# Block maxima to the query stacks' rows by eight on-chip transfers, with no store to DRAM between

## The chip, the cores and the metric

One NeuronCore of a Trainium2 chip runs the kernel. The metric is the device time of one execution in microseconds (us), as the median of several runs. Engines are named as in the profile: PE (matrix multiply; PEld are its weight loads), DVE (vector), ACT (scalar, activation functions), POOL (GpSimd) and SP (the sync engine, which here does nothing but issue transfers).

## The reference

The input x is 2048 x 512 in float32. It is normalized over each row and goes to two branches, whose results are added to x:

```python
xn = _layernorm(x)
qkv = xn @ wqkv                      # 32 heads of 16 columns each for q, k and v
scores = einsum("bhqd,bhkd->bhqk", q, k) * 16 ** -0.5
o = einsum("bhqk,bhkd->bhqd", softmax(scores), v)
return x + (o @ wo) + (gelu(xn @ w1 + b1) @ w2 + b2)
```

w1 is 512 x 1792 and w2 is 1792 x 512. The softmax needs the maximum of each query's scores over all 2048 keys; this kernel subtracts it inside the score product, and the change is about the way of these maxima into that product.

## The kernel before

**Blocks and units.** The attention is cut into 32 blocks: 8 groups of 4 heads (`NG`) times 4 blocks of 512 queries (`NQB`, `QB`). Block t has 16 units, so there are `NU` = 512. `unit()` is called once per unit u and issues, in this order on the engines' queues, pieces of several stages. For unit u it makes the first scores, queries on the partitions (`s_half`: products `pS`), and DVE reduces them to maxima (`s_max`: `mt`, line 390). For unit e = u - 19 (`LEAD`) it makes the scores again, now keys on the partitions (`e_half`: products `pT`), which ACT turns into exponentials (`pe`, line 431). One or two units behind, `v_half` multiplies these with v (`pV`). Between them stand matmuls of the dense work (`dense`: `pD`): projections, then the MLP, then the output projection. All `tiled` products carry line 171 in the profile. The queues are first in, first out, so this order is what runs.

**The stacks.** q and k lie as float16 parts in `qst` and `kst`, tiles of 128 partitions: head parts in partitions 0 to 61 and 64 to 125, and two rows more in each half, 62 and 63 (a = 0), 126 and 127 (a = 1). In `kst` these two rows hold a constant. In `qst` they hold the negated block maximum of each query as a float16 and its remainder (j = 0, 1), so that the second score product subtracts the maximum by itself. `qst` is a set of four tiles per group, two sets in turn.

**The way of the maxima.** When the last unit of block t has been reduced, `s_end` has DVE reduce `mt` to `mx` (line 358); POOL scales it and splits it into two float16 parts (lines 360 to 362). `store()`, called in the unit after it, has PE turn them by two small products (`m_turn`, line 366), ACT copy the result to `mturned`, a tile of 64 partitions x 64 elements (`m_copy`, line 371), and SP issue three transfers: `m_store` (line 347) writes `mturned` to `m_d` in DRAM, and `m_rows` (line 352), once for a = 0 and then for a = 1, reads it back into rows 62 and 63, or 126 and 127, of the block's `qst` tile. A read waits for the store's landing. The first `e_half` of block t, two units and a half after the turn, needs these rows: its product n = 1 reads the half with rows 126 and 127, the next product, n = 0, the half with rows 62 and 63.

**The opening.** Everything up to unit 18 (normalization, first projections, scores of block 0, v) is put in order by `Plan`, a planner with a cost in ns for each step, a wire time for transfers (`size`, `LAG`) and a `tail` (what still has to follow, the longest first). For block 0 it holds `m_store` as a step of 420 ns and the two `m_rows` as steps of 270 ns behind it. From unit 19 on, `unit()` alone sets the order.

**Transfers.** All transfers of this program are issued by SP, in one order. Each takes the next of eight semaphores in turn, so the ninth issued waits until the first has landed. While the first unit of a block is under way the large transfers are held back (`held`).

Of the kernel before, what the change touches and what calls it, by code (L numbers as in the profile page):

```python
# [10 lines left out]
F16 = mybir.dt.float16  # L11
# [7 lines left out]
P = 128  # L19
# [9 lines left out]
NQB = S // QB  # L29
NG = H // 4  # L30
# [9 lines left out]
LAG, E_TAIL = 3000, 8000  # L40
# [15 lines left out]
def layer_kernel(ctx: ExitStack, tc: tile.TileContext, x, wqkv, wo, w1, b1, w2, b2, out):  # L56
    nc = tc.nc
# [3 lines left out]
    def pool(stack, name, bufs=1, space=None, side=None):  # L61
        kw = {k: v for k, v in (("space", space), ("side", side)) if v is not None}
        return stack.enter_context(tc.tile_pool(name=name, bufs=bufs, **kw))
# [4 lines left out]
    dram = pool(ctx, "dram", space=DRAM)  # L68
# [4 lines left out]
    w1_d = dram.tile([NF // 2, P, 2, 2, NC, P], F16, name="w1_d")  # L73
    w2_d = dram.tile([P, 2, NF, D], F16, name="w2_d")
    acc_d = dram.tile([S, D], F32, name="acc_d")
    m_d = dram.tile([NG * NQB, 2, 2, 2, 8, P // 2], F16, name="m_d")
    ot_d = dram.tile([D, 2, S], F16, name="ot_d")
    den_d = dram.tile([NG * NQB, 2, 4, QB], F32, name="den_d")

# [5 lines left out]
    kst, qst = ([[const.tile([P, 2, QB], F16, name=f"{x}st{i}_{b}") for b in range(NQB)] for i in range(2)] for x in "kq")  # L85
# [23 lines left out]
    def banks(tag):  # L109
        k = free_banks[tag].pop(0)  # L110
        free_banks[tag].append(k)
        return bank_tile(k, tag)
# [48 lines left out]
    def given(engine, ns):  # L161
        backlog[engine] += ns
# [54 lines left out]
    class Plan:  # L217
# [7 lines left out]
        def add(self, engine, ns, fn, after=(), take=(), free=(), size=0, tail=0, gap=0):  # L225
            t = dict(gap=gap, e=engine, ns=ns, fn=fn, after=[a for a in after if a], take=take, free=free, size=size, tail=tail,
                     end=None, n=len(self.todo))
            for key in free:
                self.users.setdefault(key, []).append(t)
            self.todo.append(t)  # L230
            return t
# [111 lines left out]
            slot[0] += 1  # L343
        slot[0] = now

    def m_store(t, turned):
        nc.sync.dma_start(m_d[t].rearrange("s a j r q -> (s a j r) q"), turned)

    def m_rows(t, a):
        g, qb = divmod(t, NQB)  # L350
        dst = qst[g % 2][qb][64 * a + 62:64 * a + 64].rearrange("j p (t s q) -> j (p t) s q", s=2, q=P // 2)
        nc.sync.dma_start(dst, m_d[t, :, a].rearrange("s j r q -> j r s q"))  # L352

    def m_parts(t):

        mx = work.tile([P, 2, 8], F32, name="mx", bufs=1)
        parts = work.tile([P, 2, 2, 8], F16, name="mparts", bufs=2)
        return (lambda: nc.vector.tensor_reduce(mx.rearrange("p a r -> p (a r)"), mt_of[t].rearrange("p h t k -> p (h t) k"),  # L358
                                                axis=AX.X, op=ALU.max),
                lambda: nc.gpsimd.tensor_scalar(mx, mx, 1.0 / MROW, 0.0, op0=ALU.mult, op1=ALU.add),  # L360
                lambda: nc.gpsimd.tensor_scalar(parts[:, :, 0], mx, 1.0, 0.0, op0=ALU.mult, op1=ALU.add),
                lambda: nc.gpsimd.tensor_tensor(parts[:, :, 1], mx, parts[:, :, 0], op=ALU.subtract)), parts

    def m_turn(pt, parts):
        for s in range(2):
            nc.tensor.matmul(pt[32 * s:32 * s + 32, :64], parts[64 * s:64 * s + 64].rearrange("p a j r -> p (a j r)"),
                             nident[64 * s:64 * s + 64], start=True, stop=True)

    def m_copy(pt):
        turned = work.tile([64, 64], F16, name="mturned", bufs=2)  # L370
        nc.scalar.activation(turned, pt[:64, :64], AF.Copy)
        return turned
# [26 lines left out]
    def s_end(u):  # L399

        t, i = divmod(u, 16)
        if i < 15:
            return
        steps, parts = m_parts(t)
        for step in steps:
            step()
        given("dve", 220)

        def store():

            fresh = cur[0] is not None and 0 < sum(cur[0].at) <= 4
            pt = banks("S" if fresh else "T")
            m_turn(pt, parts)
            m_store(t, m_copy(pt))
            for a in range(2):
                m_rows(t, a)

        stores[t] = store

# [417 lines left out]
    with ExitStack() as st1:  # L837
# [45 lines left out]
        add = plan.add  # L883
# [206 lines left out]
        for w in (1, 0):  # L1090
# [5 lines left out]
            else:  # L1096
                a = add("POOL", 800, lambda wf=wf, i1=i1: nc.gpsimd.tensor_scalar(tl[wf], tl[wf], i1, 0.0, op0=ALU.mult, op1=ALU.add), [h])
                w_ready[w] = add("POOL", 1100, lambda wf=wf, hi=hi, lo=lo: nc.gpsimd.tensor_tensor(lo, tl[wf], hi, op=ALU.subtract), [a], free=[wf])
        a = add("DVE", 90, lambda: nc.vector.tensor_tensor(sexp[:, 0:1], fac0[:, 0:1], fac0[:, 1:2], op=ALU.mult), [chain])
        a = add("DVE", 90, lambda: nc.vector.tensor_scalar_mul(sexp[:, 0:1], sexp[:, 0:1], DH ** -0.5), [a])  # L1100
# [5 lines left out]
        a = add("DVE", 90, lambda: nc.vector.tensor_tensor(amv[:, 2:3], amv[:, 0:1], amv[:, 1:2], op=ALU.max), v_sum)  # L1106
# [40 lines left out]
        mkey, m_of = ("S", "m", 0), []  # L1147
        m_steps, m0 = m_parts(0)
        a = add("DVE", 220, m_steps[0], m_last)
        for step in m_steps[1:]:  # L1150
            a = add("POOL", 220, step, [a])
# [4 lines left out]

        a = add("PE", 300, turn_m, [a], take=[mkey])
        a = add("ACT", 220, lambda: m_of.append(m_copy(tl[mkey])), [a], free=[mkey])
        put = add("SP", 420, lambda: m_store(0, m_of[0]), [a], size=4)
        for k in range(2):  # L1160
            add("SP", 270, lambda k=k: m_rows(0, k), [put], size=4, tail=E_TAIL)

        for t in range(NV):
            v_tile(t)
# [17 lines left out]
        for n, src in enumerate(every[:NM]):  # L1182
            key = ("wch", "m", n)
            dst = am_all[:, 12 + n:13 + n] if n < 2 else am_all[:, n - 2:n - 1] if n < 9 else amx[:, n - 2:n - 1]
# [342 lines left out]
```

## Time and profile before

| | before |
|---|---|
| median of 3 runs | 1458.85 us (1458.36 to 1459.63) |
| the profiled execution | 1460.86 us, of which the span is 1459.0 us |
| PE busy | 1433.1 us, 98% of the span |
| DVE busy | 1350.7 us, 93% |
| ACT busy | 1258.2 us, 86% |
| POOL busy | 683.3 us, 47% |
| transfers issued by SP in this path | 32 stores, 64 reads |
| granted TensorE clock | 0.997 |

A row of the groups reads: line, engine, operation, written tile <- read tiles, count; the durations are in ns. In the timeline a row is a start in us, a duration, and what ran; a bracket at its end holds the idle time of the engine just before it and what ended it. In the waits a row is who waited for whom, the sum in us, the times, and the longest. SP rows are issue times: how long the issuing took, not when the data landed.

### The profile page before, as it was taken

The numbers are of one execution on the slowest core, as the hardware profiler recorded it, in microseconds if no ns is written. First come the engines' busy times: TensorE is split into PE (matmuls) and PEld (weight loads), VectorE is DVE, ScalarE is ACT, GpSimd is POOL, SyncE is SP. The second block draws the span as 40 slices with busy tenths as digits, with TensorE's granted clock in tenths as the row PEclk, the third lists the DMA queues.
The fourth block names the chain that finished last, engine by engine and source line by source line (L and its number), as shares of the span: only waits on it lengthen the run. The fifth ranks groups of instructions, "written<-read, shape, count | busy, mean of one in ns | idle before, by whom it ended". The sixth has DMA issues, their size and how long they took to land.

```text
span 1459.0 us, 88559 instructions
## 1 busy us (share of the span) xinstructions
PE 1433.1 (98%) x40120; PEld 946.8 (65%) x40120; DVE 1350.7 (93%) x2240; ACT 1258.2 (86%) x2399; POOL 683.3 (47%) x769
## 2 busy tenths in 40 slices
PE   7999999999999999999999999999999999999998
PEld 4336666666666666666667666666666666666665
DVE  7979999999999999999999999999999999999933
ACT  5868888888999888899988889998889999888885
POOL 3201856754589511278752127784115778212110
PEclk9999999999999999999999999999999999999999
DMA  6740564545323111121112111131102210121423
GB/s 207 219 136 28 174 203 150 165 157 162 86 88 116 51 53 38 43 86 43 46 45 79 32 45 44 41 88 45 45 25 82 56 44 20 52 63 46 126 80 116
DMA packets 113010, 124.84 MB, mean 86 GB/s; under 512 B 23292, under 2 KB 84604, under 8 KB 112632
## 3 DMA queue, kind: packets, MB, share of 16 engines
q1 hardware_dynamic: 112632, 119.18, 26.8%
q8 instruction: 313, 5.13, 1.5%
q14 instruction: 65, 0.53, 0.1%
HBM read 81.66 MB, written 37.34 MB: 82 GB/s over the span
## 4 chain that ended last, share of the span: by engine, by line
PE 85%; DMA 6%; DVE 5%; ACT 3%; issue 1%; SPq 1%; DVEq 0%; ACTq 0%
PE pD L171 26%; PE pV L171 24%; PE pT L171 18%; PE pS L171 15%; DVE mt L390 3%; DMA m_d<-mturned 3%; DMA qst<-m_d 2%; ACT pe L431 1%; PE pT L1032 1%; SPq L352 1%; DMA qk_d<-stg 0%; DMA wq<-in_A_wqkv_dram 0%; DVE bs L970 0%; DMA kst<-qk_d 0%; DMA xs<-in_A_x_dram 0%
## 5 line engine op out<-in xcount | busy, mean ns | idle before, releaser
L390 DVE TENSOR_REDUCE mt<-pS 128x1 f32<-128x512 f32 x2029 | 1279.9, 684 | 46.4 <-PE pS L171 21.3
L431 ACT ACTIVATE pe<-pT 128x512 f32<-128x512 f32 x2048 | 1106.1, 599 | 154.2 <-PE pS L171 67.8
L171 PE MATMUL pV<-pe,vv 64*32 64x512 f32 x8192 | 1084.7, 591 | 0.1
L171 PE MATMUL pT<-qst,kst 64*32 64x512 f16 x8192 | 705.2, 378 | 9.2 <-DMA qst<-m_d 8.1
L171 PE MATMUL pS<-kst,qst 62*32 62x512 f16 x8116 | 619.2, 378 | 2.0 <-DVE mt L390 1.5
L171 PEld LDWEIGHTS <-qst 62*32 62x32 f16 x8192 | 303.5, 90 | 198.4 <-issue 47.9
L171 PE MATMUL pD<-xb,wc 64*32 64x512 f16 x5376 | 362.8, 375 | 0.0
L171 PE MATMUL pD<-w_s,g 64*32 64x512 f16 x5376 | 360.5, 375 | 0.0
L171 PEld LDWEIGHTS <-kst 64*32 64x32 f16 x8192 | 277.9, 91 | 115.1 <-issue 25.8
L171 PEld LDWEIGHTS pV<-pe,vv 64*32 64x32 f32 x8192 | 239.1, 105 | 14.2 <-PE pV L171 4.6
L171 PEld LDWEIGHTS <-wc 64*32 64x32 f16 x5376 | 158.2, 91 | 45.3
L171 PEld LDWEIGHTS <-g 64*32 64x32 f16 x5376 | 160.8, 91 | 39.9
L171 PE MATMUL pD<-xt,wqk_h 64*32 64x512 f16 x2400 | 159.9, 376 | 0.0
L360 POOL TENSOR_SCALAR mx<-mx 128x16 f32<-128x16 f32 x32 | 6.5, 204 | 303.9 <-DVE mx L358 293.1
L1369 POOL TENSOR_TENSOR xa<-xa,yt 128x512 f32<-128x512 f32 x16 | 20.5, 1284 | 156.2 <-ACT yt L1367 156.2
L171 PEld LDWEIGHTS <-wqk_h 64*32 64x32 f16 x2400 | 72.4, 92 | 20.9 <-issue 2.2
L1321 POOL TENSOR_TENSOR t<-hh 128x512 f32<-128x512 f32 x56 | 58.2, 1039 | 42.6 <-ACT hh L1344 40.5
L1323 POOL TENSOR_TENSOR t<-t,hh 128x512 f32<-128x512 f32 x56 | 71.7, 1281 | 4.7
L1316 POOL TENSOR_TENSOR t<-t,hh 128x512 f32<-128x512 f32 x56 | 71.7, 1280 | 4.6
L1318 POOL TENSOR_TENSOR g<-t,g 128x512 f16<-128x512 f32 x56 | 65.2, 1164 | 4.7
L488 POOL TENSOR_TENSOR osb<-osb,rb 128x512 f32<-128x512 f32 x31 | 39.9, 1286 | 38.8 <-DMA rb<-den_d 38.3
L171 PE MATMUL pD<-wo_s,oc 64*32 64x512 f16 x816 | 54.6, 376 | 0.0
(160 smaller groups left out, 934.7 us busy)
## 6 DMA issues: line engine op xcount, KB each, us to landing
wc<-w_d SPq DMA_DIRECT2D x56, 256.0 KB
qk_d<-stg SPq DMA_DIRECT2D x32, 256.0 KB
rb<-den_d SPq DMA_DIRECT2D x124, 64.0 KB
wch<-in_B_w_dram SPq DMA_DIRECT2D x14, 512.0 KB
wch<-in_B_w_dram SPq DMA_DIRECT2D x28, 256.0 KB
w_d<-wsp SPq DMA_DIRECT2D x28, 256.0 KB
kst<-qk_d SPq DMA_DIRECT2D x64, 96.0 KB
qst<-qk_d SPq DMA_DIRECT2D x64, 96.0 KB
```

The costliest lines, as they stand in the source:

```text
L171: p = nc.tensor.matmul(*args, **kw)
L352: nc.sync.dma_start(dst, m_d[t, :, a].rearrange("s j r q -> j r s q"))
L360: lambda: nc.gpsimd.tensor_scalar(mx, mx, 1.0 / MROW, 0.0, op0=ALU.mult, op1=ALU.add),
L390: nc.vector.reduce_max(mt_of[t][:, n // 2 + n % 2 * 2, qt, kb:kb + 1], s, axis=AX.X)
L431: nc.scalar.activation(pe, st, AF.Exp, scale=scale_of[g // 2])
L488: pooled((1280, lambda: nc.gpsimd.tensor_tensor(osb, osb, rb, op=ALU.mult)), (620, lambda: nc.gpsimd.tensor_scalar(ot[:, 0], osb, 1.0, 0.0 ...
L1032: nc.tensor.matmul(tl[key], lhs, rhs, start=c + n == 0, stop=(c, n) == (NC - 1, 2))
L1316: (1280, lambda: nc.gpsimd.tensor_tensor(t1, t1, hh, op=ALU.mult)),
L1318: (1160, lambda: nc.gpsimd.tensor_tensor(g[:, 1, f, :], t1, g[:, 0, f, :], op=ALU.subtract)),
L1321: pooled((1040, lambda: nc.gpsimd.tensor_tensor(t1, hh, hh, op=ALU.mult)), (620, lambda: nc.gpsimd.tensor_scalar(t1, t1, 1.0, 1.0 / GELU_A ...
L1323: (1280, lambda: nc.gpsimd.tensor_tensor(t1, t1, hh, op=ALU.mult)),
L1369: add = lambda: nc.gpsimd.tensor_tensor(xa, xa, yt, op=ALU.add)
```

## The change

The store to DRAM and its tensor `m_d` go. `m_rows` now moves straight from `mturned` to the `qst` rows, with a transfer for each half of the queries (s) and each row (j): 8 partitions x 64 elements of `mturned` become one row of 8 pieces of 64 elements. That is four transfers for each a, eight for a block in place of three, all from the SP queue, and a = 1 goes ahead of a = 0. The product n = 1 of the first `e_half` now waits for four transfers, as does n = 0, where each waited for one; and `m_copy`, when it writes `mturned` again two blocks later, waits for the eight that read it. In the planner the steps of 420 and twice 270 ns become two of 1100 ns, with nothing between `m_copy` and them.

```diff
-    m_d = dram.tile([NG * NQB, 2, 2, 2, 8, P // 2], F16, name="m_d")
...
-    def m_store(t, turned):
-        nc.sync.dma_start(m_d[t].rearrange("s a j r q -> (s a j r) q"), turned)
-
-    def m_rows(t, a):
+    def m_rows(t, turned, a):
         g, qb = divmod(t, NQB)
-        dst = qst[g % 2][qb][64 * a + 62:64 * a + 64].rearrange("j p (t s q) -> j (p t) s q", s=2, q=P // 2)
-        nc.sync.dma_start(dst, m_d[t, :, a].rearrange("s j r q -> j r s q"))
+        for s in range(2):
+            for j in range(2):
+                row, k = 64 * a + 62 + j, 32 * s + 16 * a + 8 * j
+                dst = qst[g % 2][qb][row:row + 1].rearrange("o p (t s q) -> o s (p t) q", s=2, q=P // 2)
+                nc.sync.dma_start(dst[:, s], turned[k:k + 8])
...
             m_turn(pt, parts)
-            m_store(t, m_copy(pt))
-            for a in range(2):
-                m_rows(t, a)
+            turned = m_copy(pt)
+            for a in (1, 0):
+                m_rows(t, turned, a)
...
         a = add("ACT", 220, lambda: m_of.append(m_copy(tl[mkey])), [a], free=[mkey])
-        put = add("SP", 420, lambda: m_store(0, m_of[0]), [a], size=4)
-        for k in range(2):
-            add("SP", 270, lambda k=k: m_rows(0, k), [put], size=4, tail=E_TAIL)
+        for k in (1, 0):
+            add("SP", 1100, lambda k=k: m_rows(0, m_of[0], k), [a], size=4, tail=E_TAIL)
```

After the opening the rows of PE, DVE, ACT and POOL stand as before; only SP's differ. First SP's queue at the end of the opening and at block 1, before (each number behind a tile's name is its buffer):

```order
L913 DMA wch<-in_A_wo_dram 128x2x512 x2
L347 DMA m_d<-mturned 64x64
L1059 DMA qk_d<-stg 128x512
L352 DMA qst_0_87<-m_d 2x16x64 x2
L1058 DMA qk_d<-stg 128x2x512
L536 DMA qst_2_89<-qk_d 48x2x512 x2
L536 DMA kst_0_83<-qk_d 48x2x512 x2
L1205 DMA xn_d<-xt 256x1x512
L347 DMA m_d<-mturned 64x64
L352 DMA qst_1_88<-m_d 2x16x64 x2
L536 DMA kst_1_84<-qk_d 48x2x512 x2
```

The same stretch of SP's queue with the change:

```order
L912 DMA wch<-in_A_wo_dram 128x2x512 x2
L1058 DMA qk_d<-stg 128x512
L351 DMA qst_0_86<-mturned 1x8x64 x8
L1057 DMA qk_d<-stg 128x2x512
L535 DMA qst_2_88<-qk_d 48x2x512 x2
L535 DMA kst_0_82<-qk_d 48x2x512 x2
L1203 DMA xn_d<-xt 256x1x512
L351 DMA qst_1_87<-mturned 1x8x64 x8
L535 DMA kst_1_83<-qk_d 48x2x512 x2
```

At block 1, as at every later block, a store and two reads have become eight row transfers in the same place; at block 0 they also stand behind a store of projections (`qk_d<-stg`) that the store of the maxima stood ahead of.

The opening is also planned anew: its rows on PE, DVE and ACT are the same work in another order up to the first `e_half`. ACT's queue around the copy of block 0's maxima (line 371), before:

```order
L921 ACTIVATE wch,amx<-wch 128x1024
L371 ACTIVATE mturned<-pS 64x64
L921 ACTIVATE wch,amx<-wch 128x1024
L1044 ACTIVATE stg<-pT 128x512
L1054 ACTIVATE pf<-pT 128x512
L1129 ACTIVATE vv<-pD 128x32x16
L921 ACTIVATE wch,amx<-wch 128x1024
L1129 ACTIVATE vv<-pT 128x32x16 x2
L431 ACTIVATE pe<-pT 128x512 x14
```

And with the change, where the copy is line 370:

```order
L920 ACTIVATE wch,amx<-wch 128x1024 x4
L1043 ACTIVATE stg<-pT 128x512
L1053 ACTIVATE pf<-pT 128x512
L1128 ACTIVATE vv<-pD 128x32x16
L370 ACTIVATE mturned<-pS 64x64
L920 ACTIVATE wch,amx<-wch 128x1024 x2
L1128 ACTIVATE vv<-pT 128x32x16 x2
L430 ACTIVATE pe<-pT 128x512 x14
```

The copy has moved behind the three results of projections (`stg`, `pf`, `vv`) that it stood ahead of, and so nearer to the first exponential (`pe`), which needs the rows.

## The prediction

> **What bounds the kernel now.** I read the page's shares and its chain first, then the waits, then the timeline at two block boundaries, one late and one on time.
>
> ```profile
> span 1459.0 us, 88559 instructions
> PE 1433.1 (98%) x40120; PEld 946.8 (65%) x40120; DVE 1350.7 (93%) x2240; ACT 1258.2 (86%) x2399; POOL 683.3 (47%) x769
> PE pD L171 26%; PE pV L171 24%; PE pT L171 18%; PE pS L171 15%; DVE mt L390 3%; DMA m_d<-mturned 3%; DMA qst<-m_d 2%; ACT pe L431 1%; PE pT L1032 1%; SPq L352 1%; DMA qk_d<-stg 0%; DMA wq<-in_A_wqkv_dram 0%; DVE bs L970 0%; DMA kst<-qk_d 0%; DMA xs<-in_A_x_dram 0%
> ```
>
> PE carries the time, with DVE close behind. The chain also passes through both transfers of the maxima, 5% of the span. That share is no gain by itself: while they fly, PE has other work. What PE really loses stands in the waits.
>
> ```profile
> DVE mt L390 <- PE pS L171: 23.2, 31, 2.5
> ...
> PEld L171 <- DMA qst<-m_d: 17.0, 18, 1.5
> ...
> PE pT L171 <- DMA qst<-m_d: 8.1, 12, 1.0
> ...
> SPq L347 <- ACT mturned L371: 290.6, 32, 39.3
> SPq L352 <- DMA m_d<-mturned: 54.7, 31, 2.9
> ```
>
> PE stood still for 8.1 us in all because the rows in `qst` were not there, at 12 of the 32 blocks, and its weight loads for 17.0 us at 18. SP itself waits 54.7 us for the landings of its own stores. Here is a late boundary, first SP, then PE's weight loads and matmuls:
>
> ```profile
> 977.88 0.47 SPq L347 DMA_DIRECT2D m_d<-mturned  x1
> 981.22 1.39 SPq L352 DMA_DIRECT2D qst<-m_d  x2
> ...
> 984.06 0.10 PEld L171 LDWEIGHTS <-kst 64*32 64x32 f16 x4 [1.45 <-DMA qst<-m_d]
> ...
> 984.06 0.40 PE L171 MATMUL pT<-qst,kst 64*32 64x512 f16 x4 [0.95 <-DMA qst<-m_d]
> ```
>
> And one on time:
>
> ```profile
> 760.72 2.60 SPq L679 DMA_DIRECT2D xb<-xn_d  x3
> 770.52 0.50 SPq L347 DMA_DIRECT2D m_d<-mturned  x1
> 772.25 1.37 SPq L352 DMA_DIRECT2D qst<-m_d  x2
> ...
> 775.34 0.42 PE L171 MATMUL pT<-qst,kst 64*32 64x512 f16 x4
> ...
> 775.64 0.41 PE L171 MATMUL pT<-qst,kst 64*32 64x512 f16 x4
> ```
>
> Counted from the start of the store, PE comes to the product n = 1 after 4.82 us (775.34 - 770.52) and to n = 0 after 5.12. At the late boundary n = 1 starts at 6.18, so 1.36 late, of which PE idles 0.95: the first 0.41 are covered by matmuls still running. The difference between the two is the store: its landing lets the reads go after 3.34 us there and 1.73 here. The stretches from one reduction of maxima to the next, with these two kinds of boundary:
>
> ```profile
> 726.10:768.30 42.20, 41.27 (x1233) 28.80 (x1222) 40.30 (x66) 37.02 (x71) 22.18 (x25) 1.00 0.14 39
> 768.30:809.00 40.70, 40.70 (x1230) 28.95 (x1222) 40.24 (x67) 35.61 (x68) 7.46 (x9) 1.00 0.27 79
> ```
>
> The first has a late boundary (PE busy 41.27 of 42.20), the second none (PE 40.70 of 40.70, DVE 40.24). So a late boundary costs its PE idle time or a little more, and a block without one is at the limit of PE and nearly of DVE: nothing below that is to be had.
>
> **The change, part by part.** *The removed store and its wait.* Every PE wait on `qst<-m_d` goes: 8.1 us by the PE row. DVE's waits for `pS` (23.2) bound the gain from above, since they hold other causes too; I take 8.1.
>
> *The eight transfers.* This is the term that decides. They start when the store started, run one behind the other on SP, and land some time after their issue ends. The landing: from the end of the store's issue (770.52 + 0.50) to the reads' start is 1.23 us; from the end of the second read's issue (981.22 + 1.39) to PE's start 1.45, with 32 pieces of 64 elements each. A row transfer has 8 pieces, so I take 1.2. With a pitch p from one issue to the next, the rows for n = 1 are there at 4p + 1.2, those for n = 0 at 8p + 1.2. No row of before has this transfer; its nearest:
>
> ```profile
> L469 SPq DMA_DIRECT2D den_d<-osb x124: 215/244/537, 148.9 to 1407.7; - x124
> ...
> L347 SPq DMA_DIRECT2D m_d<-mturned x32: 466/476/527, 87.3 to 1396.9; - x32
> ...
> L495 SPq DMA_DIRECT2D ot_d<-ot x124: 570/594/2279, 197.6 to 1430.6; - x124
> ...
> L352 SPq DMA_DIRECT2D qst<-m_d x64: 603/658/793, 89.9 to 1399.8; - x64
> ```
>
> The medians are 0.24 us for one whole row, 0.48 for plain partitions of 64 elements, 0.59 and 0.66 where source and destination are cut differently. Two reads take 1.39, so each costs 0.04 more than its own time. Then p is 0.28, 0.52, 0.63 or 0.70, and the rows for n = 0 come at 3.4, 5.3, 6.2 or 6.8 us, against a need of 5.12. For n = 1 the worst is 4.0 against 4.82: it never waits, which is the use of taking a = 1 first. n = 0 is late by 0, 0.2, 1.1 or 1.7; less 0.41 of cover PE idles 0, 0, 0.7 or 1.3 us a block, over 31 blocks (block 0 is in the opening) 0, 0, 22 or 39 us. The new transfer is cut differently on its two sides (8 partitions become one row) but has only 8 pieces, so I put it between the store and the `ot_d` row, nearer to the store: p = 0.53. Then n = 0 comes at 5.44, 0.32 late. That lies within the cover, so PE idles for nothing by this count; but running dry still costs some overlap, between 0 and 0.32 a block, 0 to 10 us. I take 4.
>
> *What stands behind.* SP's next transfers at the on-time boundary started 3.15 us after the store (772.25 + 1.37 + 0.04 - 770.52 at the earliest), and now start at 8p = 4.2; at the late boundary they started at 4.8. No PE wait on one of them is among the large rows, so 0. The semaphores: the eight take all eight, so the last can wait for a transfer issued before the first. At the on-time boundary the last large ones were issued by 763.32 (760.72 + 2.60), 7 us earlier, and the late store took 3.3 us to land: 0.
>
> *More waits on ACT and PE.* The copy on ACT now waits for up to eight landings of two blocks ago, PE for four in place of one:
>
> ```profile
> L371 ACTq EVENT_SEMAPHORE  x28: 17/17/17, 179.8 to 1396.1; - x28
> ```
>
> At 17 ns each, up to four more in front of the copy delay it by under 0.1 us a block, which lies within the bounds of p. On PE the same price for four more at a block's start is 0.07 us, 2 us in all at most; nothing below zero, as they only add. I take 0, because the weight loads ahead of them have idle time to give on most boundaries.
>
> *The opening.* It is the same work in another order.
>
> ```profile
> 87.02 0.22 ACT L371 ACTIVATE mturned<-pS 64x64 f16<-64x64 f32 x1 [0.95 <-PE pS L366]
> ...
> 89.83 0.61 ACT L1129 ACTIVATE vv<-pD 128x512 f32<-128x512 f32 x1
> ...
> 87.26 0.53 SPq L347 DMA_DIRECT2D m_d<-mturned  x1
> ...
> 90.00:100.00 10.00, 8.84 (x122) 3.43 (x125) 7.69 (x13) 3.94 (x8) 1.16 (x1) 1.00 0.34 107
> ...
> 96.60 0.39 PE L171 MATMUL pT<-qst,kst 64*32 64x512 f16 x4
> 98.15 0.41 PE L171 MATMUL pS<-kst,qst 62*32 62x512 f16 x8 [1.16 <-DVE mt L390]
> 98.37 0.40 PE L171 MATMUL pT<-qst,kst 64*32 64x512 f16 x4
> ```
>
> Before, n = 1 of block 0 came 9.3 us after the store's start and n = 0 11.1. The copy now stands behind three more ACT results, of which this `vv` is the last. It ended at 90.44, so measured on the old opening the copy comes 3.4 us later than 87.02. That leaves n = 1 at 5.9 us against 4p + 1.2 = 3.3, and n = 0 at 7.7 against 5.44: no wait. PE idles 1.16 us in the last 10 us of the opening, so a better order can give about that and a worse one take as much: 0, with 1.5 to either side.
>
> *The sum.* -8.1 + 4 + 0 = -4 us. The profiled execution took 1460.86 (span 1459.0 and 1.9 around it), so it would take 1457; the median of the runs, 1458.85, is 2.0 lower, and with the same 4 off gives 1455.
>
> **The rivals.** *The issue of eight becomes the wait (slower).* SP issues one after the other, and n = 0 waits at every block, also where before it was on time. It decides from a pitch of about 0.59: there PE idles 8 x 0.59 + 1.2 - 5.12 - 0.41 = 0.39 us a block, 12 in all, 4 more than the 8.1 won. At the `ot_d` row's pitch it is +14, 1473; at that of `qst<-m_d` +31, 1490. For it speaks that this row, with the same destination, is the dearest; against it that its transfers have four times the pieces. The Trainium skill (DMA: Bandwidth & Descriptors, "Rules for kernel authors") says of many small transfers that one should coalesce them, since below 64 KB one pays mostly overhead; by that rule three transfers in place of eight are right and this change goes the wrong way, to the 1473 to 1490 just worked out. The trace agrees so far that the issue price hardly follows the bytes (0.48 us for 8 KB, 0.66 for 4 KB). Against the rule stands that the three are two landings in a row and the eight only one.
>
> *A wash.* With p between 0.56 and 0.59, or with the uncovered loss at its full 0.3 us a block, what n = 1 wins n = 0 gives back: 1456 to 1462. The large row of DVE's waits speaks for less loss, as `pS` now stands ahead of the late product in PE's queue and DVE is fed.
>
> *The whole gain.* With p at or under 0.5, near the store's row or below, no boundary waits: 1458.85 - 8.1 = 1451, and 1449 with a good opening.
>
> **How the numbers follow.** A change under 0.2% (2.9 us) can't be told from none. The forecast, with the whole gain as its better end (1448 to 1456), has 0.45; the wash 0.20; the slow issue 0.35. So faster 0.45, same 0.20, slower 0.35. The forecast's own range is 1448 to 1456. The full range goes from 1448 to 1478, the slow issue up to a pitch of 0.65; that leaves out its upper third (0.12) and a little below.
>
> **What would show it.** In the profile after, the row of `qst<-mturned` gives the issue time (forecast 0.49 us) and its timeline the pitch. No boundary should wait at n = 1, which is the first `pT` of a block; a wait there means a landing far over 1.2 us or a held semaphore. A wait that is there should name `qst<-mturned` ahead of the second `pT`, be alike at all blocks, and make DVE wait less than before. The opening is right if the first `pT` still starts at 95 to 98 us. The forecast is wrong if the pitch is over 0.59, or if stretches like 726 to 768 do not come down towards 40.7 although PE no longer waits.

## The result, and the profile after

The changed kernel takes 1507.15 us, median of 4 runs (1505.59 to 1512.22), against 1458.61 (1458.12 to 1459.63) for the kernel before: a ratio of 1.0338, 95% interval 1.0311 to 1.0365. It is 48.5 us slower, where the prediction said 4 faster, and it lies outside the range (1448 to 1478). The page of the changed kernel, with the rows that answer to those shown of before:

```profile
span 1503.9 us, 88901 instructions
PE 1444.2 (96%) x40120; PEld 951.2 (63%) x40120; DVE 1353.3 (90%) x2240; ACT 1262.6 (84%) x2399; POOL 683.3 (45%) x769
PE pD L170 23%; PE pV L170 22%; PE pT L170 16%; PE pS L170 13%; SPq L351 9%; DMA qst<-mturned 4%; ACT pe L430 2%; DVE mt L389 1%; PE pT L1031 1%; PE pD L1031 0%; DMA wq<-in_A_wqkv_dram 0%; DVE bs L969 0%; DVE sd L971 0%; ACT mturned L370 0%; DMA xs<-in_A_x_dram 0%
```

DVE and ACT do the same work as before, in a longer span. New in the chain is SP's queue on line 351, the issue of the eight, with 9% of the span, and 4% for their landing. Before, the store and reads had 1% of issue (`SPq L352`) and 5% of landing. The waits say who pays:

```profile
PE pT L170 <- DMA qst<-mturned: 40.2, 31, 2.3
...
DVE mt L389 <- PE pS L170: 36.5, 35, 5.4
DVE mt L389 <- PE pT L170: 33.2, 40, 2.7
```

PE waits for the rows 31 times, at every block end but the opening's, 40.2 us in all (before 8.1 us, 12 times). DVE's waits for PE rise too, from 23.2 us for `pS` and 5.4 for `pT`. The row of the transfers, and one block end on SP and PE:

```profile
L351 SPq DMA_DIRECT2D qst<-mturned x256: 624/628/1552, 94.2 to 1445.7; - x128
```

```profile
790.79 5.47 SPq L351 DMA_DIRECT2D qst<-mturned  x8
796.31 0.57 SPq L678 DMA_DIRECT2D xb<-xn_d  x1
...
795.61 0.41 PE L170 MATMUL pT<-qst,kst 64*32 64x512 f16 x4
795.68 0.59 PE L170 MATMUL pS<-kst,qst 62*32 62x512 f16 x8
797.33 0.40 PE L170 MATMUL pT<-qst,kst 64*32 64x512 f16 x4 [1.07 <-DMA qst<-mturned]
```

Eight issues take 5.47 us, 0.68 each. The first `pT`, n = 1, starts 4.82 us after the first issue (795.61 - 790.79) and waits for nothing. The second, n = 0, starts after 6.54 us, which is 1.07 us after the end of the eighth issue. This is the block that was on time before the change. From one reduction of maxima to the next it took 40.70 us then, and takes 42.00 now, with PE busy for 40.93 of them:

```profile
788.60:830.60 42.00, 40.93 (x1230) 28.53 (x1219) 40.34 (x66) 35.56 (x68) 7.46 (x9) 1.00 0.27 77
```

### The profile page after: what moved, and what is told of

The parts are those of the page before. It is cut to its first block, busy times and chain, and to the rows that moved or that the text cites. A ratio compares the mean times of both kernels' runs of the same rounds, so it can differ in the third digit from the quotient of the medians.

```text
span 1503.9 us, 88901 instructions
## 1 busy us (share of the span) xinstructions
PE 1444.2 (96%) x40120; PEld 951.2 (63%) x40120; DVE 1353.3 (90%) x2240; ACT 1262.6 (84%) x2399; POOL 683.3 (45%) x769
## 4 chain that ended last, share of the span: by engine, by line
PE 77%; SPq 9%; DMA 4%; ACT 4%; DVE 3%; issue 2%; ACTq 0%; DVEq 0%
PE pD L170 23%; PE pV L170 22%; PE pT L170 16%; PE pS L170 13%; SPq L351 9%; DMA qst<-mturned 4%; ACT pe L430 2%; DVE mt L389 1%; PE pT L1031 1%; PE pD L1031 0%; DMA wq<-in_A_wqkv_dram 0%; DVE bs L969 0%; DVE sd L971 0%; ACT mturned L370 0%; DMA xs<-in_A_x_dram 0%
## 5 line engine op out<-in xcount | busy, mean ns | idle before, releaser
L170 PE MATMUL pT<-qst,kst 64*32 64x512 f16 x8192 | 708.9, 378 | 41.5 <-DMA qst<-mturned 40.2
L170 PE MATMUL pS<-kst,qst 62*32 62x512 f16 x8116 | 626.3, 378 | 2.3 <-DVE mt L389 1.7
L170 PEld LDWEIGHTS <-qst 62*32 62x32 f16 x8192 | 307.0, 91 | 198.1 <-issue 49.8
L170 PEld LDWEIGHTS pV<-pe,vv 64*32 64x32 f32 x8192 | 237.1, 105 | 11.9 <-PE pV L170 4.3
L170 PEld LDWEIGHTS <-g 64*32 64x32 f16 x5376 | 160.2, 92 | 41.7 <-issue 0.4
```

The source lines that it names most:

```text
L170: p = nc.tensor.matmul(*args, **kw)
```

## The experiments

The theory, A: SP issues the eight one behind the other at 0.68 us each, so the rows of n = 0 are there 6.5 us after the first issue, and PE pays the whole lateness at each block end. The rivals: the new order of the opening makes the loss (B); a transfer inside the on-chip memory is itself slow to land, however many there are (C); taking a = 1 first is what hurts (D); a transfer costs by its pieces, or all pass one after another whoever issues them (E). Unless said otherwise the kernels keep the opening in the order of before (a step of 420 and two of 270 on SP), so that on every engine but SP the work stands in its old order. The ratios are to the kernel before on the same chip.

**Eight transfers, old opening.** The edit to the changed kernel:

```
+        put = add("SP", 420, lambda: None, [a], size=4)
         for k in (1, 0):
-            add("SP", 1100, lambda k=k: m_rows(0, m_of[0], k), [a], size=4, tail=E_TAIL)
+            add("SP", 270, lambda k=k: m_rows(0, m_of[0], k), [put], size=4, tail=E_TAIL)
```

> The eight transfers of the changed kernel, with the opening's planner steps as before the change (a step of 420 and two of 270 on SP), so that every engine's instructions stand in the order of the kernel before and only the transfers differ. Theory A (the loss is the serial issue of eight at 0.67 us, paid at each of the block ends, and the new order of the opening adds 3.7 us): about 1503, 3 to 4 us under the changed kernel's 1507; SP's issue of the eight stays at 0.62 to 0.68 us each, and the rows that the second transpose reads are there 6.5 to 6.8 us after the first issue. Rival B (the planner's new order, not the transfers, makes the loss): within 5 us of the time before, 1459.

Measured: 1503.53 us (1499.59 to 1505.09), ratio 1.0288 (1.0269 to 1.0308). PE waits 41.7 us for the rows, again 31 times. B falls: the loss is there without the new opening.

**Four transfers, one for a row.** The copy on ACT is split in two, so that 8 partitions hold 128 elements of one row:

```
-        turned = work.tile([64, 64], F16, name="mturned", bufs=2)
-        nc.scalar.activation(turned, pt[:64, :64], AF.Copy)
+        turned = work.tile([32, 2, 64], F16, name="mturned", bufs=2)
+        for s in range(2):
+            nc.scalar.activation(turned[:, s], pt[32 * s:32 * s + 32, :64], AF.Copy)
...
+                nc.sync.dma_start(dst, turned[k:k + 8].rearrange("k s q -> k (s q)"))
```

> The same way inside the on-chip memory with half of the transfers: the turned parts are laid out [32, 2, 64] by two ACT copies, and each of four transfers fills one row (8 pieces of 128 elements). Order of the opening as before the change. Theory A (the number of issues on one queue): four at 0.65 us and 1.2 us of landing make 3.8 us, about 0.2 more for the second copy, under the 5.1 us that the second transpose leaves: no wait on the rows at the block ends, time 1449 to 1454, under the kernel before. Rival C (a transfer inside the on-chip memory is itself slow to land, the count does not matter): the rows still arrive after 6 us, time 1490 to 1505.

Measured: 1450.10 us (1448.1 to 1451.0), ratio 0.9932 (0.9915 to 0.9949). No PE wait for the rows is left. The way inside the on-chip memory is faster than the one over DRAM once there are four transfers; C falls.

**Two transfers.** The same tile, 16 partitions to two rows at a time:

```
+        dst = qst[g % 2][qb][64 * a + 62:64 * a + 64].rearrange("j p (t x) -> j (p t) x", x=P)
+        nc.sync.dma_start(dst, turned[16 * a:16 * a + 16].rearrange("k s q -> k (s q)"))
```

> As the kernel with four, but two transfers in a block, each from 16 partitions into two rows. Theory A: two issues and a landing make 2.5 to 3 us, no wait on the rows, 1449 to 1453, equal to the kernel with four within 2 us, since both are inside the need. Rival C: the rows late as with eight, 1490 to 1505. If the issue time grows with the bytes or pieces of one transfer and not with their count, the two issues take 1.3 us each and four take 0.65, and the two kernels are alike in all else.

Measured: 1449.01 us (1448.28 to 1450.03), ratio 0.9921 (0.9905 to 0.9938), the same as with four. Each issue now moves 4 KB in place of 1, in 16 pieces of 128 elements in place of 8 of 64, and takes no longer to speak of. This is the row of SP's transfers with two, where the median was 628 ns with eight:

```profile
L348 SPq DMA_DIRECT2D qst<-mturned x64: 611/672/832, 89.8 to 1386.9; - x64
```

**Four transfers with the pieces of eight.** The kernels so far differ also in the pieces that a block's rows are cut into. This one keeps the tile, its single copy and the 64 pieces of 64 elements of the changed kernel, and only joins two rows in one transfer:

```
-            for j in range(2):
-                row, k = 64 * a + 62 + j, 32 * s + 16 * a + 8 * j
-                ...
-                nc.sync.dma_start(dst[:, s], turned[k:k + 8])
+            k = 32 * s + 16 * a
+            nc.sync.dma_start(dst[s], turned[k:k + 16])
```

> The turned tile, its one copy and the pieces in memory are those of the kernel with eight (64 pieces of 64 elements a block), but the two rows of one half go out in one transfer of 16 pieces, so four transfers a block. Order of the opening as before the change. Theory A (the count of issues on SP): no wait on the rows, 1448 to 1452, the same as the kernel with four rows. Rival E (the cost of a transfer goes with its pieces, so the issue of each doubles to 1.2 us or the landing comes later): the rows 6 us after the first issue, 1490 to 1503.

Measured: 1449.62 us (1447.5 to 1450.93), ratio 0.9938 (0.9921 to 0.9954). The first form of E falls: at equal pieces and bytes, half the issues take the 54 us of the kernel with eight away. Its transfers, and the block end that was shown above of the changed kernel:

```profile
L350 SPq DMA_DIRECT2D qst<-mturned x128: 596/612/832, 88.5 to 1386.1; - x128
```

```profile
759.94 2.74 SPq L350 DMA_DIRECT2D qst<-mturned  x4
...
764.76 0.41 PE L170 MATMUL pT<-qst,kst 64*32 64x512 f16 x4
...
765.12 0.40 PE L170 MATMUL pT<-qst,kst 64*32 64x512 f16 x4
```

```profile
759.90:800.60 40.70, 40.70 (x1234) 29.04 (x1218) 40.25 (x67) 35.62 (x68) 7.41 (x10) 1.00 0.28 79
```

n = 1 starts again at 4.82 us and n = 0 at 5.18, with no wait ahead of either, and the stretch (here from the first issue of this block to that of the next) is 40.70 us with PE busy throughout. So 5.18 is what the block leaves, and eight transfers, with 6.54, were late by 1.36.

**Six and seven transfers: is lateness hidden?** The tile of the four transfers, and some of its rows sent in two halves: both rows of a = 0 for six, one of a = 1 as well for seven.

```
         for j in range(2):
             row, k = 64 * a + 62 + j, 16 * a + 8 * j
+            if a:                 # with seven: if a and j == 0
                 ...
                 nc.sync.dma_start(dst, turned[k:k + 8].rearrange("k s q -> k (s q)"))
+            else:
                 ...
+                for s in range(2):
+                    nc.sync.dma_start(dst[:, s], turned[k:k + 8, s])
```

> Six transfers a block: the rows of the first transpose by two, those of the second by four. Theory A with all lateness paid: the rows are there at 6 x 0.676 + 1.13 = 5.19 us after the first issue against 5.0 to 5.1 that the block leaves, late by 0.1 to 0.2 us, 31 times: 1452 to 1457. Theory A with 0.41 us of lateness hidden behind matmuls still running (as the prediction had it): nothing lost, 1449 to 1451. Rival C (count does not matter): above 1485.

> Seven transfers a block: three, then four. The rows at 7 x 0.676 + 1.13 = 5.86 us, late by 0.8 us. All lateness paid: 31 x 0.8 = 25 us above the kernel with four, 1473 to 1477. With 0.41 us hidden: 12 us above it, 1461 to 1464.

Measured: six 1468.53 us (1465.46 to 1471.39), ratio 1.0057 (1.0041 to 1.0074); seven 1489.26 (1485.35 to 1492.8), ratio 1.0203 (1.0178 to 1.0229). Both are 11 to 12 us above even the reading in which all lateness is paid. The first issue and the second `pT` of the same block end in the kernel with four rows, with six and with seven; the `pT` starts 4.96, 5.30 and 6.00 us after the issue:

```profile
761.52 2.79 SPq L350 DMA_DIRECT2D qst<-mturned  x4
...
766.48 0.40 PE L170 MATMUL pT<-qst,kst 64*32 64x512 f16 x4
```

```profile
770.94 1.45 SPq L351 DMA_DIRECT2D qst<-mturned  x2
...
776.24 0.40 PE L170 MATMUL pT<-qst,kst 64*32 64x512 f16 x4
```

```profile
781.25 0.72 SPq L351 DMA_DIRECT2D qst<-mturned  x1
...
787.25 0.40 PE L170 MATMUL pT<-qst,kst 64*32 64x512 f16 x4 [0.74 <-DMA qst<-mturned]
```

With the two copies of this tile the block leaves 4.96 us, since the kernel with four rows has no wait there. For this block, timed from its first `pe` to that of the next (eight with the old opening):

| transfers | start of n = 0, us | block leaves | late | PE idle ahead of it | block, us | over 40.68 |
|---|---|---|---|---|---|---|
| 4 (rows) | 4.96 | 4.96 | 0 | 0 | 40.68 | 0 |
| 4 (pieces) | 5.18 | 5.18 | 0 | 0 | 40.68 | 0 |
| 6 | 5.30 | 4.96 | 0.34 | 0.04 | 41.04 | 0.36 |
| 7 | 6.00 | 4.96 | 1.04 | 0.74 | 41.71 | 1.03 |
| 8 | 6.54 | 5.18 | 1.36 | 1.07 | 42.05 | 1.37 |

The block grows by the lateness, to 0.02 us, and not by the idle time, which is 0.3 less in each row. No part of the lateness is hidden. At six, PE is idle for 0.04 us and the block still loses 0.36. The sums over blocks 1 to 31 say the same. Against the kernel with four rows, n = 0 is late by 38 us in all with seven, and the blocks are 43 us longer, with 28 us of PE idle ahead of these products. Against the one with four pieces, eight transfers (old opening) are late by 52 us and longer by 56, with 42 us of idle.

The expectations were too low because they took 5.0 to 5.1 us for what the block leaves, where the two copies make it 4.96, and because at some blocks one issue takes far longer (last section) or the last rows land later. With six, n = 0 starts 2.6 to 3.3 us after the last issue at blocks 3, 13 and 19, where it is 1.16 at the block above. What delays these landings wasn't tested.

**The order of the halves.** First with eight transfers:

```
-            for a in (1, 0):
+            for a in range(2):
```

> Eight transfers, old order of the opening, and the rows of the second transpose first, those of the first transpose last. Theory A (rows there at 8 x 0.676 + 1.13 = 6.54 us, all lateness paid): the first transpose, which stands at 4.6 to 4.8 us, is now the one that waits, late by 1.8 us against 1.36 for the second one before: 0.4 to 0.5 us more in each of 31 blocks, 1514 to 1521. Rival D (which half goes first makes no difference, since both transposes are needed for the work behind): 1501 to 1506.

Measured: 1516.34 us (1513.89 to 1521.01), ratio 1.0393 (1.0369 to 1.0417). On the same block end the first `pT` now waits, and starts 6.56 us after the first issue (798.03), 1.74 late:

```profile
804.59 0.40 PE L170 MATMUL pT<-qst,kst 64*32 64x512 f16 x4 [1.49 <-DMA qst<-mturned]
```

That is 0.38 us more lateness than with a = 1 first; 31 times, 12 us, and the medians stand 12 to 13 apart. Then the other way round, a = 1 first in the kernel before, over DRAM (the opening's two reads are turned round as well):

```
-            for a in range(2):
+            for a in (1, 0):
```

> The kernel before with its store to DRAM kept, and only the order of the two reads of the rows turned round (the rows that the first pT reads come first). Theory A: the first reader's wait at n=1 (before: part of 8.1 us of waits on the rows) goes down by one issue (0.7 us), the second has 0.3 us more slack: 1453 to 1458. Rival D (the order of the two is itself what hurts in the changed kernel): slower than before by more than 5 us.

Measured: 1456.03 us (1454.3 to 1459.12), ratio 0.9973 (0.9963 to 0.9982). PE's waits for the rows go from 8.1 to 2.4 us. D falls on both: the order is worth 4 us to the kernel before, and is not what made the change slow.

**The opening alone.** The kernel before, its store and reads kept, with the two SP steps of the opening sized as in the changed kernel:

```
-        put = add("SP", 420, lambda: m_store(0, m_of[0]), [a], size=4)
...
+        for k in (1, 0):
+            add("SP", 1100, lambda k=k: both(k), [a], size=4, tail=E_TAIL)
```

> The kernel before with its store to DRAM and its two reads, and only the opening's two SP steps sized 1100 each, so that every compute engine's order is that of the changed kernel. Theory A (the new order of the opening costs its own 4 to 5 us, as the difference between 1.0338 and 1.0288 of the time before says): 1463 to 1465 against 1459 to 1460. Rival (the opening's order is worth nothing by itself, the difference comes from the transfers there): within 1.5 us of the kernel before.

Measured: 1460.43 us (1457.89 to 1463.9), ratio 1.0009 (0.9999 to 1.0019). So the changed kernel was run again beside the kernel with eight transfers and the old opening:

> The changed kernel once more, beside the kernel with eight transfers and the old order of the opening, on one chip. The first two comparisons gave 1.0338 and 1.0288 of the time before. If the new order of the opening costs 4 to 5 us with these transfers, the two kernels stand 4 to 5 us apart again; if it costs about 1 us, as it did over the DRAM way (1.0009), they stand under 2.5 us apart.

> Eight transfers with the old order of the opening: 1.026 to 1.031 of the time before. 4 to 5 us under the changed kernel if the opening's order matters by itself, under 2.5 us if it does not.

Measured: 1507.75 us (1504.36 to 1511.01), ratio 1.0334 (1.0317 to 1.0351), and 1504.27 (1503.16 to 1511.58), ratio 1.0320 (1.0298 to 1.0343). The medians stand 3.5 us apart, between the two readings, and the intervals overlap. By the ratios the first pair of comparisons (1.0338 and 1.0288) stands 0.5% apart, 7 us, and this one 0.14%, 2 us. The new order of the opening costs between nothing and 7 us of the 48; more is not settled.

**Half of the issues on ACT.**

```
-                nc.sync.dma_start(dst[:, s], turned[k:k + 8])
+                (nc.sync if a else nc.scalar).dma_start(dst[:, s], turned[k:k + 8])
```

> The same eight transfers, but the four for the second transpose are issued by ACT behind its copy of the turned parts, at the same time as the four on SP. Theory A (the loss is the serial issue on one queue): the rows are there 4 x 0.676 + 1.13 = 3.8 us after the first issue and no transpose waits for them; ACT loses 4 x 0.6 = 2.5 us at each block end, of which its idle time (188 us in the kernel before, 5.9 us a block) hides part: 1450 to 1480. Rival E (the transfers themselves are slow, or all pass one after another whoever issues them): waits on the rows stay as with eight on SP, 1500 or more.

Measured: 1552.00 us (1550.1 to 1556.2), ratio 1.0644 (1.0623 to 1.0664), far above A's range. It lies where E's does (1500 or more), but E's sign, the waits on the rows, is not there. One block end on SP and on ACT, then PE's wait:

```profile
809.75 2.79 SPq L351 DMA_DIRECT2D qst<-mturned  x4
...
809.52 0.21 ACT L370 ACTIVATE mturned<-pT 64x64 f16<-64x64 f32 x1
809.76 3.14 ACTq L351 DMA_DIRECT2D qst<-mturned  x4
812.95 2.06 ACT L430 ACTIVATE pe<-pT 128x512 f32<-128x512 f32 x4 [3.22 <-DMA qst<-mturned]
...
PE pT L170 <- ACT pe L430: 70.6, 31, 2.7
```

The two queues issue side by side. PE waits for the rows nowhere; it waits for ACT, which issues for 3.14 us in place of its exponentials (the 3.22 us that the row of `pe` counts as idle are this issuing). ACT's issues take 96 us in blocks 1 to 31 and PE waits 70.6 for it, so ACT's idle time, 5.9 us a block, hid little; the expectation was wrong to count on it. Part of the 102 us over the kernel with four may be the granted clock, 0.983 over this span against 0.997; how much isn't shown. When the rows landed isn't seen either: PE comes to n = 0 no sooner than 7.2 us after the first issue, when eight on one queue (6.54) would be there too. So the second form of E, that the transfers pass one after another whoever issues them, stays open.

## Why the prediction was wrong

The mechanism was seen, and named as a rival: n = 0 waits at all blocks because SP issues eight in a row. Two steps of the sum had the wrong size.

*The pitch.* The prediction put p at 0.53 us, between the store's row and that of `ot_d`, because the new transfers have few pieces. It is 0.68 (5.47 / 8). The right row was there: `qst<-m_d`, which fills the same rows of a `qst` tile and gave 0.70. That both write `qst` can't be the reason, for `qst<-qk_d` has a median of 0.43 us; what sets the time isn't shown. The row's pieces were the reason to go below it, and the pieces count for little: 0.61 to 0.71 us at the median in all kernels with on-chip transfers, with 8 or 16 pieces of 64 or 128 elements, 1 to 4 KB.

*The cover.* The prediction took 0.41 us off the lateness, since matmuls were still running when PE ran out of new ones, and charged a lateness within the cover with "between 0 and 0.32 a block". The table shows that a lateness of 0.34 costs 0.36. The matmuls behind the late one start later by the whole lateness, whatever still runs. The two stretches quoted for the kernel before couldn't tell this, since they are of different blocks; a late block has to be read against the same block on time. The first of the two, late at n = 1, took 42.20 us; the same block takes 41.10 with four joined transfers (716.6 to 757.7). It grew by 1.10 us for a lateness of 1.13 (5.92 against 4.79), where PE idled 0.93.

With p = 0.68 and the cover kept, the prediction's formula gives 8 x 0.684 + 1.2 - 5.12 - 0.41 = 1.14 us a block, 35 in all, less 8.1: +27. The cover, 0.41 x 31, adds 13. The longer issues add 4.4: seven of them in the trace, 8.8 us together where 0.63 each would be 4.4. That makes +44, against 44.9 between the two spans and 48.5 between the medians.

That this comes so close is partly luck, since two errors in it nearly cancel. The gain of 8.1 is PE's idle time again: counted from the start of the store or the first issue, n = 1 of the kernel before starts later than with four joined transfers by 11.9 us in all, and the two spans are 13.3 us apart (1459.0 and 1445.7). And the opening, put at 0 with 1.5 us to either side, is left out: up to the first `pe` of block 1 the trace of the changed kernel is 5.1 us longer than that of the four. From there on its blocks are 53.0 us longer, for a lateness of 51.3. These terms, -13.3 + 5.1 + 53.0, give 44.8 of the 44.9.

*What held.* The landing was put at 1.2 us after the last issue; the block above shows 1.07. n = 1 never waits for the rows. The wait names `qst<-mturned` ahead of the second `pT` at all 31 blocks, but it isn't alike everywhere: 0.77 to 2.30 us. The need was put at 5.12 and is 5.18. The semaphores cost nothing that shows: the pitch of eight, 0.68, is that of four (2.74 / 4). The time without a late boundary was put at 1449 to 1451, and is 1449 to 1450 with four and two transfers, 9 to 12 us under the kernel before. The rival of the slow issue had +31 at a pitch of 0.70; its cover was the main thing wrong with it. The wash at 0.56 to 0.59, and with it the point from which the slow issue decides, fall with the cover.

*What else failed.* DVE was to wait less; it waits 36.5 us for `pS` and 33.2 for `pT`, where it waited 23.2 and 5.4, since every late product delays the ones behind it. In the opening the first `pT` was to start at 95 to 98 us; it starts at 100.26 in the trace of the changed kernel and at 97.28 in that of its second run. The two differ in the granted clock (0.97 and 1.00, the third number from the right), as these stretches up to block 0's reduction show, the first of the changed kernel, the second of its second run:

```profile
40.00:92.50 52.50, 49.31 (x408) 19.03 (x406) 43.06 (x79) 37.74 (x70) 10.24 (x9) 0.97 0.70 213
```

```profile
40.00:89.50 49.50, 46.32 (x396) 18.29 (x395) 41.76 (x75) 36.87 (x68) 10.25 (x9) 1.00 0.68 213
```

Up to block 1's reduction the opening takes 134.0 us before, 137.7 in the first of the two traces and 134.7 in the second. So the 3.7 us by which it was longer in the first are not all the order's.

*The rule.* The Trainium skill (DMA: Bandwidth & Descriptors, "Rules for kernel authors"), which asks to coalesce many small transfers, was weighed in the prediction and set aside for the shorter chain of landings. The runs bear it out: two transfers with the bytes of eight are 54 us faster than eight (1449.01 against 1503.53), and the cost of one hardly follows its bytes. But three over DRAM were not the best either: joined transfers and the short chain go together.

## What to carry to other kernels

Count the issues on one queue before the bytes: the last of n transfers is there after n issue times and one landing. Take the issue time from the row of the profile that is nearest in form (here the one that fills the same rows, 0.66 us, and not a mean between unlike rows), and compare the result with what the consumer leaves, to a tenth of a microsecond. When an engine that bounds the kernel starts its next piece late, count the whole lateness, not the idle time in its row. If two rows can go out in one transfer, joining them turned this change from 3.4% slower to 0.6 to 0.8% faster than the kernel before.

## What the runs showed of the hardware

Some issues of row transfers on SP take 1.0 to 1.7 us in place of 0.63, at much the same few blocks in the kernels with six to eight transfers. In the traces with eight transfers there are 7 to 10 of them, and each stands beside one transfer of 16 KB on the queue of kind "instruction" that started at most 0.5 us ahead of it. One of them, and the row of that queue between 235.5 and 237 us (its columns are packets, MB and share of the 16 engines' time):

```profile
235.64 1.26 SPq L351 DMA_DIRECT2D qst<-mturned  x1
```

```profile
q8 instruction: 1, 0.02, 4.1%
```

Such a transfer by itself isn't enough: one stands as near ahead of 29 of the 249 other issues of the changed kernel, which take 0.62 to 0.90 us.

In the changed kernel and in the first run of eight transfers with the old opening, seven of the long issues are the same transfers by their number on SP (the 193rd, 419th, 593rd, 615th, 766th, 911th and 1060th). With six and with seven transfers long issues fall in blocks 8, 14, 19, 24 and 29 again, but at other numbers (in block 14 the 587th and the 601st, in place of the 615th). So the long issues keep their place in the schedule and not their count on SP, which speaks against SP's loading of its own program at fixed counts. What makes them long stays open. With four transfers, one for a row, there are two (1.18 and 1.61 us), and with four joined from the pieces of eight none (the longest issue is 0.83 us).
